# Two chunk pairs inverted side by side before the main loop, and the wide lane products on VectorE

## The chip, the cores and the metric

One core of one Trainium2 chip. The metric is the device time of one execution in microseconds; several runs are given by their median.

## What is computed

The program is a linear attention with a state matrix per head, followed by a dense feed-forward block and a mixture of eight experts. Cut to what matters:

```python
# attention: batch 4, 8 heads (32 "lanes"), 768 steps, head size 40
for t in range(S):
    y[t] = r[t] @ state
    Sa = state @ a[t]
    state = state * w[t] - outer(Sa, b[t]) + outer(v[t], k[t])
# dense block on 3072 tokens of width 320
h = x @ w_in                          # 320 -> 2048
x = where(h > 0, h, exp(min(h, 0)) - 1) @ w_out
# experts: softmax gate, best of 8, up to 768 tokens each
y = relu(x_e @ w1[e]) @ w2[e];  out = gate * y
```

## The kernel before, in words

**Tiling.** The 768 steps are cut into 24 chunks of 32 (`NCH`), taken as 12 pairs (`NP`). Within a chunk the recurrence becomes matrix products, if a 32 x 32 unit triangular matrix per lane is inverted. A pair has 64 such matrices (2 chunks x 32 lanes). Two pairs make a group of 128 steps, so there are six groups.

**`lanes` (L126)** makes, for one group, running products of the decay w inside each chunk and scales a, b and k by them. Tiles are 128 partitions (32 lanes x 4 chunks) by 32 steps by 40. The narrow steps (L166, L169, L190, L193) take 160 or 320 elements per partition, the three wide products (L174, L196, L201) 1280. For group 0 the engine `eng` is VectorE (DVE) and the tiles are separate (`room`); for groups 1 to 5 it is GpSimd (POOL), one tile `lx` takes a, b and k in turn, and loads and stores are issued by POOL. L174 runs on POOL for all six groups. The results go to DRAM.

**`pre` (L269)** of a pair: three times it takes a token tile (`turn`, L242: TensorE transposes, copies off PSUM, then the next load of the list `order`, L118), multiplies them (L288), masks the product on DVE into `TM` (L294) and stores that to `Td` in DRAM (L299), once per chunk.

**`inverse` (L308)** of a pair loads `Td` back lane-wise (L315), and in 31 steps j builds the inverse in `UL`, all on DVE: an outer product of n x m elements with n = j // 2 + 1 and m = 30 - j (L323), a multiply-add of one column (L328), an add of the outer product (L330). The result goes to `Ud` (L334) and back as `UT`, in eight loads (L339).

**`chain` (L371)** of a chunk is the serial part. Its second step (L407) multiplies by `UT`; the state that it leaves (L428, L429) is what the next chunk starts from. At its end `put` (L583) transposes the attention output into the tokens of the dense block.

**`Moe1.weights`, called conv (L494)** reads the dense weights in 40 items (per 5 items, 3 of w_in and 2 of w_out), each converted by one or two ScalarE (ACT) and five DVE instructions (L515 to L519, L480, L481); a w_out item also has transposes and small products on TensorE (L556, L560). `Moe1.block(p)` (L593) is the dense block on the 256 tokens of pair p.

**The order.** A scheduling program orders each engine's instructions by priority; `ahead` raises a generator's priority, `weave` deals generators out in a ratio. `issue_after(ins)` queues what is issued inside it behind `ins`, on the engine of `ins` alone. Each engine then runs its instructions in that fixed order. `start` (L1118) is lanes 0, `pre(0)`, `inverse(0)`, lanes 1; it is woven with 9 steps of conv. Then `pre(1)` is woven with the rest of conv, whose DVE instructions stand behind the last add of `inverse(0)` (L1152). Then comes the main loop over p (L1154): the chains of pair p, `inverse(p + 1)`, `pre(p + 2)`, a part of the lanes of a later group, and `block(p - 1)`. After it the experts follow.

Of the kernel before, what the change touches and what calls it, by code (L numbers as in the profile page):

```python
# [38 lines left out]
class Attention:  # L39
# [31 lines left out]
    def setup(self, ident, psum):  # L71
# [47 lines left out]
        for p in range(-2, NP):  # L119
            if p >= 0:  # L120
                self.order.append(("r", p))
            if p + 2 < NP:
                self.order += [("a", p + 2), ("bk", 2 * p + 4), ("bk", 2 * p + 5)]
        self.loaded = self.taken = self.banks = 0

    def lanes(self, g, eng, eng2=None, room=None):  # L126

# [3 lines left out]
        nc = self.nc  # L131
        eng2 = eng2 or eng
        W, la, wd = self.t("W"), self.t("lx"), self.t("WCd")
# [39 lines left out]
        nc.vector.tensor_copy(wd[:, 64:104], W[:, 32, :])  # L173
        nc.gpsimd.tensor_tensor(la, la, W[:, 0:32, :], ALU.mult)  # L174
        store(self.scr_A[g], la)
        if not room:
            store(self.scr_W[g], W[:, 0:32, :])
            load(W[:, 0:32, :], "w")
            load(lb, "b")
        ps = self.psum("p")  # L180
        nc.tensor.transpose(ps[0:104, 0:128], wd, self.ident)
# [10 lines left out]
        for q in range(3, -1, -1):  # L192
            eng.tensor_tensor(  # L193
                Vq[:, q], Vq[:, q], V[:, 8 * q + 8, :].unsqueeze(1).to_broadcast([128, 8, 40]), ALU.mult)
            yield
        eng2.tensor_tensor(lb, lb, V[:, 1:33, :], ALU.mult)  # L196
        store(self.scr_BK[g][:, 0:C], lb)
        if not room:
            load(lk, "k")
        yield  # L200
        self.scaled = eng2.tensor_tensor(lk, lk, V[:, 1:33, :], ALU.mult)  # L201
        store(self.scr_BK[g][:, C:2 * C], lk)
# [17 lines left out]
    def load_tok(self):  # L220

        if self.loaded == len(self.order):
            return
        kind, i = self.order[self.loaded]
        t = self.t("tok", self.loaded)
        self.loaded += 1
        for hg in range(2):
            rows = t[64 * hg:64 * hg + 64]
            if kind == "r":
                self.load_heads(rows, self.src["r"], hg, 64 * i, 64)  # L230
            elif kind == "a":
                for cc in range(2):
                    self.nc.sync.dma_start(
                        rows[32 * cc:32 * cc + 32, :, 0:40],
                        self.of(self.scr_A[i // 2], 2 * (i % 2) + cc, 16 * hg, 16).rearrange("l s d -> s l d"))
            else:

                with self.tc.issue_after(self.returned.ins) if i == 4 else ExitStack():
                    self.last = self.nc.sync.dma_start(
                        rows[:, :, 0:40], self.of(self.scr_BK[i // 4], i % 4, 16 * hg, 16).rearrange("l x d -> x l d"))  # L240
# [67 lines left out]
    def inverse(self, p):  # L308
# [27 lines left out]
        for cc in range(2):  # L336
            for b in range(4):
                h = 32 * cc + 8 * b
                self.returned = self.nc.sync.dma_start(  # L339
                    self.t("UT", 2 * p + cc)[32 * b:32 * b + 32], self.Ud[p][:, h:h + 8, :])  # L340
        yield

    def load_pv(self, c):
# [27 lines left out]
    def chain(self, c, put):  # L371
# [88 lines left out]
        if c + 2 < NCH:  # L460
            self.load_pv(c + 2)
        nc.scalar.copy(xt[:, 320:384], xt[:, 256:320])
        if not last:
# [20 lines left out]
class Moe1:  # L484
# [80 lines left out]

    def begin_x(self, ctx, i):
        pool = ctx.enter_context(self.tc.tile_pool(name=f"moe1_x{i}", bufs=1))
        self.xH.append(pool.tile([128, 3, 256], F32R, name=f"xH{i}"))
        self.xL.append(pool.tile([128, 3, 256], F32R, name=f"xL{i}"))
# [505 lines left out]
def body(ctx, tc, r, k, v, w, a, b, w_in, w_out, w_gate, w1, w2, out, capacity=768):  # L1075
# [26 lines left out]
    moe1.begin_x(st["moe1"], 1)  # L1102
    moe1.begin(st["moe1"], psum)
    put = moe1.put_x(ident, psum)
    stage = ExitStack()
    pool = stage.enter_context(tc.tile_pool(name="stage", bufs=1))
    steps = lambda t: t.rearrange("p (s d) -> p s d", d=D)
# [10 lines left out]
    def start():  # L1118
        lanes = att.lanes(0, nc.vector, room=room)
        for _ in range(25):  # L1120
            next(lanes)
            yield
        pre = att.pre(0)
        drain(lanes)
        yield from pre
        inverse = att.inverse(0)
        next(inverse)
        with tc.issue_after(att.last.ins):
            att.load_pv(0)
            att.load_bkd(0)  # L1130
            att.load_wp(0)
            att.load_pv(1)
        yield
        drain(att.lanes(1, nc.gpsimd))
        yield from inverse
# [13 lines left out]
    with tc.issue_after(att.landed.ins):  # L1149
        next(conv)  # L1150
    weave((first, 20), (behind(att.scaled.ins, some(conv, 9)), 20))
    weave((ahead(tc, att.pre(1), 1000), 10), (behind(att.inverted.ins, conv), 40))  # L1152
    lanes = None
    for p in range(NP + 1):  # L1154
        gens = []
        if p < NP:
            gens.append((ahead(tc, chained(att.chain(2 * p, put), att.chain(2 * p + 1, put)), 2000), 32))
            if p % 2 == 0:
                lanes = att.lanes(p // 2 + 2, nc.gpsimd) if p // 2 + 2 < NP // 2 else iter(())
            if p + 1 < NP:  # L1160
                gens.append((ahead(tc, att.inverse(p + 1), 1500), 20))
            if p + 2 < NP:
                gens.append((ahead(tc, att.pre(p + 2), 1500), 20, 6))
            gens.append((ahead(tc, some(lanes, 14) if p % 2 == 0 else lanes, 500 if p == 0 else 2000), 14))
        if p == 1:
            stage.close()
            moe1.begin_x(stage, 2)
        if p == NP:
# [74 lines left out]
```

## Time and profile before

| | us |
|---|---|
| median of 3 runs | 1213.22 (1212.05 to 1215.55) |
| the profiled execution, whole | 1217.03 |
| its span, first to last instruction | 1215.3 |
| PE (TensorE) matmul busy in the span | 1027.2 (85%) |
| DVE busy | 822.6 (68%) |
| ACT busy | 599.1 (49%) |
| POOL busy | 256.1 (21%) |

Busy times are of the profiled execution. PE's granted clock is 0.904 of full speed on average. An engine's share is over the whole span, and the program passes through stages with different limits, so stretches are read one by one.

### The profile page before, as it was taken

The page shows a single profiled execution, that of the slowest core. Times are in us where ns is not written, and L with a number is a line of the kernel's source. Part 1 is how long each engine was busy: PE and PEld are TensorE (multiplying, and loading weights), DVE is VectorE, ACT ScalarE, POOL GpSimd, SP SyncE. Part 2 cuts the span into 40 slices and gives each one's busy share as a digit, 9 for nine tenths or more (in the row PEclk, how much of TensorE's full clock was granted, in tenths as well). Part 3 has the DMA queues.
Part 4 walks back from the last instruction along what each step waited for, and adds up shares of the span by engine and source line. Part 5 has one row for each costly group of instructions (what it writes and reads, how often), then busy time and mean ns, then how long its engine had stood idle before and what let it go on. Part 6 is the DMA issues. An engine that isn't in the chain of part 4 may idle for free.

```text
span 1215.3 us, 35896 instructions
## 1 busy us (share of the span) xinstructions
PE 1027.2 (85%) x14568; PEld 933.5 (77%) x14568; DVE 822.6 (68%) x2755; ACT 599.1 (49%) x1499; POOL 256.1 (21%) x314
## 2 busy tenths in 40 slices
PE   0454588888988989889999979999998798989995
PEld 0344478777976988779888879888988697979995
DVE  6676798998679576968596949686445456545541
ACT  1432246564654655556556655656655345434420
POOL 5355543410035100400000000000001232323311
PEclk9855669899998989899999989999989999989998
DMA  6887667663356544452616351522131165544210
GB/s 217 205 196 217 188 166 173 194 132 65 62 103 176 104 67 81 106 104 51 108 31 101 58 104 30 91 50 44 27 88 25 39 188 159 164 134 124 82 45 22
DMA packets 294400, 131.27 MB, mean 108 GB/s; under 512 B 261560, under 2 KB 276032, under 8 KB 294224
## 3 DMA queue, kind: packets, MB, share of 16 engines
q1 hardware_dynamic: 276672, 76.39, 32.2%
q0 software_dynamic: 10064, 37.39, 9.7%
q10 hardware_dynamic: 7488, 15.09, 4.1%
q8 instruction: 117, 1.92, 0.7%
q14 instruction: 59, 0.48, 0.1%
HBM read 99.13 MB, written 31.00 MB: 107 GB/s over the span
## 4 chain that ended last, share of the span: by engine, by line
PE 41%; DVE 27%; DMA 19%; ACT 5%; issue 5%; SPq 2%; POOL 1%; ACTq 0%; POOLq 0%; DVEq 0%
PE ps_h L609 8%; PE ps_c L383 4%; DVE inv L328 4%; DVE inv L330 4%; DVE ut L323 3%; DMA out_dram<-ys,ids 3%; DMA inv<-Td 3%; PE ps_o L623 3%; PE ps_o L625 3%; PE ps_o L624 3%; PE ps_c L931 2%; DMA Td<-keep 2%; PE ps_h L931 2%; DMA r<-in_moe_w_dram 2%; DMA Ud<-inv 2%
## 5 line engine op out<-in xcount | busy, mean ns | idle before, releaser
L480 ACT CAST gH<-e 128x256 fp32r<-128x256 f32 x192 | 77.2, 405 | 116.7 <-DVE e L615 102.0
L623 PE MATMUL ps_o<-woH,gH 128*128 128x328 f32 x384 | 129.5, 340 | 5.2 <-ACT gH L480 4.5
L728 POOL DMA_INDIRECT list<-ids,idx x24 | 24.1, 1004 | 498.4 <-DVE idx L724 306.8
L624 PE MATMUL ps_o<-woL,gH 128*128 128x328 f32 x384 | 125.7, 329 | 0.0
L625 PE MATMUL ps_o<-woH,gL 128*128 128x328 f32 x384 | 120.7, 336 | 4.9 <-DVE gL L481 4.8
L615 DVE SCALAR_TENSOR_TENSOR e<-e,ps_h 128x256 f32<-128x256 f32 x184 | 76.2, 415 | 69.0 <-ACT e L614 65.5
L609 PE MATMUL ps_h<-xH,wiH 128*128 128x256 f32 x368 | 113.0, 308 | 10.4 <-DVE e L615 6.6
L323 DVE TENSOR_TENSOR ut<-inv 128x30 f32<-128x30 f32 (+4 forms) x360 | 93.2, 259 | 29.0 <-DMA inv<-Td 28.6
L609 PE MATMUL ps_h<-xL,wiH 128*128 128x256 f32 x368 | 108.6, 295 | 0.0
L609 PE MATMUL ps_h<-xH,wiL 128*128 128x256 f32 x368 | 108.5, 296 | 0.0
L328 DVE SCALAR_TENSOR_TENSOR inv<-inv 128x1 f32<-128x1 f32 (+15 forms) x372 | 101.5, 273 | 0.6
L330 DVE TENSOR_TENSOR inv<-inv,ut 128x30 f32<-128x30 f32 (+4 forms) x360 | 99.7, 277 | 0.2
L481 DVE TENSOR_TENSOR gL<-e,gH 128x256 fp32r<-128x256 f32 x192 | 81.3, 426 | 26.7 <-ACT gH L480 23.3
L253 PE MATMUL ps_p<-ident,tok 128*104 128x128 f32 x288 | 55.0, 320 | 49.4 <-DMA tok<-scr_A 24.8
L613 ACT ACTIVATE e<-ps_h 128x256 f32<-128x256 f32 x184 | 70.3, 384 | 53.4 <-PE ps_h L609 33.9
L609 PEld LDWEIGHTS ps_h<-xH,wiH 128*128 128x128 f32 x368 | 73.7, 201 | 15.0 <-DVE e L615 9.5
L623 PEld LDWEIGHTS ps_o<-woH,gH 128*128 128x128 f32 x384 | 76.8, 200 | 7.7 <-ACT gH L480 5.5
L614 ACT ACTIVATE e<-e 128x256 f32<-128x256 f32 x192 | 79.1, 417 | 4.3
L625 PEld LDWEIGHTS ps_o<-woH,gL 128*128 128x128 f32 x384 | 73.6, 199 | 7.9 <-DVE gL L481 7.2
L253 PEld LDWEIGHTS ps_p<-ident,tok 128*104 128x104 f32 x288 | 35.9, 148 | 56.4 <-issue 25.5
L624 PEld LDWEIGHTS ps_o<-woL,gH 128*128 128x128 f32 x384 | 77.1, 201 | 0.5
L609 PEld LDWEIGHTS ps_h<-xL,wiH 128*128 128x128 f32 x368 | 74.1, 201 | 0.1
(323 smaller groups left out, 2867.5 us busy)
## 6 DMA issues: line engine op xcount, KB each, us to landing
r<-in_moe_w_dram SPq DMA_DIRECT2D x15, 640.0 KB
tok<-scr_BK SPq DMA_DIRECT2D x48, 160.0 KB
BKd<-scr_BK SPq DMA_DIRECT2D x48, 160.0 KB
r<-in_moe_w_dram SPq DMA_DIRECT2D x7, 1024.0 KB
W<-in_w_dram POOLq DMA_DIRECT2D x10, 640.0 KB, 6.3
scr_BK<-lx POOLq DMA_DIRECT2D x10, 640.0 KB, 3.5
inv<-Td SPq DMA_DIRECT2D x24, 256.0 KB
raw<-in_moe_w_out_dram ACTq DMA_DIRECT2D x16, 320.0 KB
```

The source lines that it names most:

```text
L253: self.nc.tensor.transpose(ps[0:104, 128 * j:128 * j + 128], t[:, 2 * q:2 * q + 2, :].rearrange("p a e -> p (a e)")[:, 0:104], self.ident,)
L323: nc.vector.tensor_tensor(tv, TL[:, j:j + 1, j + 2:32].to_broadcast([128, n, m]), UL[:, 0:n, j:j + 1].to_broadcast([128, n, m]), ALU.mult,)
L328: nc.vector.scalar_tensor_tensor(col, UL[:, 0:n, j], TL[:, j, j + 1:j + 2], col, ALU.mult, ALU.add)
L330: self.inverted = nc.vector.tensor_tensor(UL[:, 0:n, j + 2:32], UL[:, 0:n, j + 2:32], tv, ALU.add)
L480: split.last = nc.scalar.copy(H, x)
L481: return (low or nc.vector).tensor_tensor(L, x, H.bitcast(F32), ALU.subtract)
L609: nc.tensor.matmul(h, l, r, start=i == 0, stop=i == len(seq) - 1)
L614: nc.scalar.activation(e, e, AF.Exp, scale=-1.0)
L615: nc.vector.scalar_tensor_tensor(e, e, -1.0, h, ALU.add, ALU.max)
L623: nc.tensor.matmul(o, gH[:, ts], self.woH[:, f], start=f == 0, stop=False)
L624: nc.tensor.matmul(o, gH[:, ts], self.woL[:, f], start=False, stop=False)
L625: nc.tensor.matmul(o, gL[:, ts], self.woH[:, f], start=False, stop=f == NF - 1)
```

## The change

- The opening runs `pre(0)` and `pre(1)`, and then one `inverses` for both pairs: the partitions hold chunk lanes as before, and a new free dimension q holds the two pairs. Per step j there are one outer product and one add, each over both pairs, and two multiply-adds of a column, one for each pair (its factor is a per-partition scalar). The 8 KB tile `twice` holds the input of both and is given up after conv.
- The results of pair 0 are stored and loaded first; of pair 1, the `UT` of its first chunk is loaded in the opening and that of its second in chain 0 (three `UT` buffers).
- Lanes 1 stand after the loads of `inverses` in the program; the load of token tile ("a", 2) is held until then. Their transposition takes a PSUM bank of another tag.
- In the opening 14 steps of conv are woven in, not 9; the other items stand behind the last add of `inverses`, on DVE. `inverse(1)` leaves the main loop, and from p = 1 on the loop is as before.
- The three wide products are issued to DVE in all groups; the narrow steps, loads and stores of groups 1 to 5 stay on POOL.
- Some pools change sides, and the pool of the dense block opens after `twice` is given up.

```diff
-    def lanes(self, g, eng, eng2=None, room=None):
+        self.hold = True
+    def lanes(self, g, eng, room=None):
...
-        nc.gpsimd.tensor_tensor(la, la, W[:, 0:32, :], ALU.mult)
+        nc.vector.tensor_tensor(la, la, W[:, 0:32, :], ALU.mult)
...
-        ps = self.psum("p")
+        ps = self.psum("o" if g == 1 else "p")
...
-        eng2.tensor_tensor(lb, lb, V[:, 1:33, :], ALU.mult)
+        nc.vector.tensor_tensor(lb, lb, V[:, 1:33, :], ALU.mult)
...
-        self.scaled = eng2.tensor_tensor(lk, lk, V[:, 1:33, :], ALU.mult)
+        self.scaled = nc.vector.tensor_tensor(lk, lk, V[:, 1:33, :], ALU.mult)
...
+        if self.hold and (kind, i) == ("a", 2):
+            return
...
+    def inverses(self, room):
+        nc = self.nc
+        TL = room.rearrange("p (q a b) -> p q a b", q=2, a=32)
+        UL = self.inv[:, 0:1024].rearrange("p (q a b) -> p q a b", q=2, a=16)
+        ut = [self.inv[:, 1024 + 256 * i:1280 + 256 * i] for i in range(2)]
+        nc.vector.memset(self.inv[:, 0:1024], 0.0)
+        for i in range(2):
+            half = slice(64 * i, 64 * i + 64)
+            for q in range(2):
+                self.last = self.nc.sync.dma_start(TL[half, q], self.Td[q])
+                nc.vector.memset(self.inv[half, 512 * q:512 * q + 512][:, i::34], 1.0)
+        yield
+        for j in range(31):
+            n, m = j // 2 + 1, 30 - j
+            if m:
+                tv = ut[j % 2][:, 0:2 * n * m].rearrange("p (q a b) -> p q a b", q=2, a=n)
+                nc.vector.tensor_tensor(
+                    tv, TL[:, :, j:j + 1, j + 2:32].to_broadcast([128, 2, n, m]),
+                    UL[:, :, 0:n, j:j + 1].to_broadcast([128, 2, n, m]), ALU.mult,
+                )
+            for q in range(2):
+                col = UL[:, q, 0:n, j + 1]
+                nc.vector.scalar_tensor_tensor(
+                    col, UL[:, q, 0:n, j], TL[:, q, j, j + 1:j + 2], col, ALU.mult, ALU.add)
+            if m:
+                rest = UL[:, :, 0:n, j + 2:32]
+                self.inverted = nc.vector.tensor_tensor(rest, rest, tv, ALU.add)
+            if j % 2 == 1:
+                yield
+        for p in range(2):
+            for i in range(2):
+                self.nc.sync.dma_start(
+                    self.Ud[p].rearrange("(a i) l t -> i l a t", i=2)[i], UL[64 * i:64 * i + 64, p])
+            for cc in range(2 - p):
+                self.load_ut(p, cc)
+        yield
...
+        if c == 0:
+            self.load_ut(1, 1)
...
-    moe1.begin(st["moe1"], psum)
+    moe1.psum = psum
...
+    twice = beside.enter_context(tc.tile_pool(name="beside", bufs=1)).tile([128, 2048], F32, name="twice")
...
         yield from pre
-        inverse = att.inverse(0)
+        yield from att.pre(1)
+        inverse = att.inverses(twice)
         next(inverse)
         with tc.issue_after(att.last.ins):
...
-        yield
-        drain(att.lanes(1, nc.gpsimd))
+            drain(att.lanes(1, nc.gpsimd))
+            att.hold = False
+            att.load_tok()
+        yield
         yield from inverse
...
-    weave((first, 20), (behind(att.scaled.ins, some(conv, 9)), 20))
-    weave((ahead(tc, att.pre(1), 1000), 10), (behind(att.inverted.ins, conv), 40))
+    weave((first, 26), (behind(att.scaled.ins, some(conv, 14)), 20))
+    drain(behind(att.inverted.ins, conv))
+    beside.close()
+    moe1.begin(st["moe1"], psum)
...
-            if p + 1 < NP:
+            if p > 0 and p + 1 < NP:
                 gens.append((ahead(tc, att.inverse(p + 1), 1500), 20))
```

## Rows read from the trace of the kernel before

**Rows 1.** Busy time by engine in three stretches; us, PE, PEld, DVE, ACT, POOL, PE clock, DMA.

```profile
104.00:188.00 84.00, 60.60 (x951) 52.61 (x952) 66.63 (x196) 31.12 (x84) 37.08 (x46) 0.62 0.70 185
188.00:284.00 96.00, 82.01 (x1286) 72.17 (x1284) 85.70 (x256) 58.65 (x166) 28.89 (x33) 0.93 0.67 163
284.00:420.00 136.00, 121.51 (x2159) 109.66 (x2158) 105.23 (x370) 71.96 (x188) 31.94 (x37) 0.91 0.48 103
```

**Rows 2.** The chain that ended last, 104 to 188 us; start us, us, what.

```profile
106.94 8.99 DMA Td<-keep
116.50 8.85 DMA inv<-Td
```

**Rows 3.** What PE waited for, 104 to 284 us; us in total, times, longest.

```profile
PE ps_c L383 <- DVE pv L414: 7.3, 3, 5.1
PE ps_c L383 <- DMA UT<-Ud: 6.9, 1, 6.9
PE ps_c L253 <- DVE ST L428: 5.7, 2, 5.0
```

**Rows 4.** The timeline in the opening, wide products of group 0; start us, us, what.

```profile
12.53 2.89 POOL L174 TENSOR_TENSOR lx<-lx,W 128x1280 f32<-128x1280 f32 x1 [0.24 <-DVE W L169]
12.60 3.31 DVE L172 COPY WCd<-W 128x40 f32<-128x40 f32 x1
...
19.50 1.49 DVE L196 TENSOR_TENSOR keep<-keep,inv 128x1280 f32<-128x1280 f32 x1
```

**Rows 5.** The timeline around `pre(0)`, `pre(1)` and the first inversion.

```profile
60.43 0.68 DVE L294 TENSOR_TENSOR keep<-ps_p,m_tm 128x512 f32<-128x512 f32 x1
...
64.70 1.10 PE L253 MATMUL ps_p<-ident,tok 128*104 128x128 f32 x4
...
70.55 0.19 DVE L323 TENSOR_TENSOR ut<-inv 128x30 f32<-128x30 f32 x1 [5.38 <-DMA inv<-Td]
...
72.22 1.98 PE L288 MATMUL ps_p<-Abd,BKT 104*64 104x64 f32 x32 [0.68 <-ACT BKT L275]
```

**Rows 6.** The timeline of steps of the first inversion, its last instruction, the first use.

```profile
75.64 0.20 DVE L323 TENSOR_TENSOR ut<-inv 128x54 f32<-128x54 f32 x1
...
76.02 0.23 DVE L323 TENSOR_TENSOR ut<-inv 128x78 f32<-128x78 f32 x1
...
81.52 0.29 DVE L323 TENSOR_TENSOR ut<-inv 128x128 f32<-128x128 f32 x1
81.72 0.23 DVE L328 SCALAR_TENSOR_TENSOR inv<-inv 128x8 f32<-128x8 f32 x1
81.87 0.28 DVE L330 TENSOR_TENSOR inv<-inv,ut 128x128 f32<-128x128 f32 x1
82.07 0.28 DVE L323 TENSOR_TENSOR ut<-inv 128x120 f32<-128x120 f32 x1
...
92.86 0.24 DVE L328 SCALAR_TENSOR_TENSOR inv<-inv 128x16 f32<-128x16 f32 x1
...
104.30 0.31 PE L383 MATMUL ps_c<-X,UT 32*32 32x40 f32 x2 [6.87 <-DMA UT<-Ud]
```

**Rows 7.** POOL's groups to 520 us; busy us, mean ns, idle before them, what ended it.

```profile
L193 POOL TENSOR_TENSOR W<-W 128x320 f32<-128x320 f32 x20 | 17.9, 897 | 112.9 <-DVE W L187 64.6 <-DVE at L721 47.0
...
L201 POOL TENSOR_TENSOR lx<-lx,W 128x1280 f32<-128x1280 f32 x5 | 14.7, 2931 | 18.3 <-DMA lx<-in_k_dram 18.2
```

**Rows 8.** The dense block 0 ends: PE's timeline.

```profile
283.93 0.31 PE L625 MATMUL ps_o<-woH,gL 128*128 128x328 f32 x1
```

**Rows 9.** PE and PEld busy of L560, then of L556, 104 to 284 us; as rows 1.

```profile
104.00:284.00 180.00, 15.24 (x78) 14.40 (x78) 0.78 0.68 173
...
104.00:284.00 180.00, 7.63 (x36) 4.33 (x36) 0.78 0.68 173
```

**Rows 10.** The chain that ended last, whole span: DVE pieces; start us, us, what.

```profile
367.96 2.80 DVE inv L330
...
508.71 3.10 DVE inv L328
```

More of the change, by code (lines that the diff above doesn't have):

```diff
@@ L124, in setup @@
         self.loaded = self.taken = self.banks = 0
-    def lanes(self, g, eng, eng2=None, room=None):
+        self.hold = True
+    def lanes(self, g, eng, room=None):
         nc = self.nc
-        eng2 = eng2 or eng
         W, la, wd = self.t("W"), self.t("lx"), self.t("WCd")
@@ L336, in inverse, with load_ut @@
         for cc in range(2):
[L337 to L340, printed above, removed]
+            self.load_ut(p, cc)
         yield
+    def inverses(self, room):
[32 more added lines that the diff above has]
+            for cc in range(2 - p):
+                self.load_ut(p, cc)
+        yield
+    def load_ut(self, p, cc):
+        for b in range(4):
+            h = 32 * cc + 8 * b
+            self.returned = self.nc.sync.dma_start(
+                self.t("UT", 2 * p + cc)[32 * b:32 * b + 32], self.Ud[p][:, h:h + 8, :])
     def load_pv(self, c):
@@ L564, in weights, with begin_x @@
                 yield
-    def begin_x(self, ctx, i):
-        pool = ctx.enter_context(self.tc.tile_pool(name=f"moe1_x{i}", bufs=1))
+    def begin_x(self, ctx, i, **kw):
+        pool = ctx.enter_context(self.tc.tile_pool(name=f"moe1_x{i}", bufs=1, **kw))
         self.xH.append(pool.tile([128, 3, 256], F32R, name=f"xH{i}"))
@@ L1102, in body @@
     moe1.begin_x(st["moe1"], 1)
-    moe1.begin(st["moe1"], psum)
+    moe1.psum = psum
     put = moe1.put_x(ident, psum)
     stage = ExitStack()
-    pool = stage.enter_context(tc.tile_pool(name="stage", bufs=1))
+    pool = stage.enter_context(tc.tile_pool(name="stage", bufs=1, side="right"))
+    beside = ExitStack()
+    twice = beside.enter_context(tc.tile_pool(name="beside", bufs=1)).tile([128, 2048], F32, name="twice")
     steps = lambda t: t.rearrange("p (s d) -> p s d", d=D)
@@ L1166, in body @@
             stage.close()
-            moe1.begin_x(stage, 2)
+            moe1.begin_x(stage, 2, side="right")
         if p == NP:
```

## The prediction
> **What bounds the kernel now.** I read the page's busy times first and then the stretches, because the shares over the whole span (PE 85%, DVE 68%) hide that the limit moves. In rows 1 the reader sees three stages. From 104 to 188 us, where chains 0 and 1 run before the dense block has started, PE is busy for 60.6 of 84 us at a granted clock of 0.62, and DVE for 66.6. From 188 to 284 us, the dense block 0, DVE is busy for 85.7 of 96 us and PE for 82.0, now at 0.93. From 284 on PE is busy for nine tenths and more [rows 1]. So up to 284 us DVE is the engine that is nearly full, and PE runs with holes and partly at half clock.
>
> Second I read what PE waited for there [rows 3]: 7.3 us for DVE's scaling of pv, 5.7 us for DVE's update of ST, 6.9 us for the return of the first inverse. Third the chain that ended last: between 107 and 125 us it is no engine at all but the second pair's trip through DRAM, 8.99 us out and 8.85 us back [rows 2], and then `inverse(1)` on DVE. Fourth the timeline beside a wide POOL product: a DVE copy that begins at 12.60, with POOL's product running from 12.53 to 15.42, takes 3.31 us [rows 4]. Later pieces of 2.8 to 3.1 us of single small inversion instructions stand in the chain that ended last for the same reason; four of them come after 360 us, the first and the last are shown [rows 10].
>
> **The change, part by part.** The sum is made against the profiled execution, 1217.0 us whole; the median of the runs, 1213.2, is 3.8 us below it, and at the end I take the difference off the median.
>
> *Wide products.* One on DVE takes 1.49 us [rows 4], one on POOL 2.93 [rows 7], and while that runs DVE gets one instruction through, in about 2.8 to 3.1 us. So each move takes some 1.4 us off DVE, though it adds an instruction there. In the opening it is direct: 3.31 us become 1.49 and a short copy, which I put at 0.2, about the length of the small column instruction [rows 6]. Gain 1.6, and I take 1.5, as the token loads behind it are DMAs.
>
> On this point the Trainium skill speaks against the change: Perfetto Trace Analysis, section Optimizing Scalar/DVE Operations, says that when DVE is saturated, moving some work to ScalarE or even GpSimd may make sense, and adds that DVE and GpSimd share a port, so that moves between these two might not help. By its first half each move back to DVE would cost the 1.49 us; the 3.31 us copy [rows 4] stands for the second half, and by that row the sum has a gain.
>
> *The inversion starts later.* The mask of `pre(0)`'s second chunk ends at 60.43 + 0.68 = 61.1 us [rows 5]. Less 1.5 from the opening and 1.5 for the wide product of group 1, which lies in that stretch: 58.1. `pre(1)` then runs undivided. From its first transposes at 64.70 to the end of its first L288 group at 72.22 + 1.98 = 74.2 it took 9.5 us, then a mask of 0.7. The second chunk has one token tile instead of two (half of 72.22 - 64.70, 3.8 us), the products of 2.0 and a mask of 0.7. Together 58.1 + 9.5 + 0.7 + 6.5 = 74.8. Out to DRAM and back took 70.55 - 61.1 = 9.4 us [rows 5]; four loads instead of two, I take 10.5. The inversion starts at about 85.3 us instead of 70.55. The other bound is the slow trip, 17.8 us [rows 2]: 93. I keep near the lower one, since conv is held back to 14 items and little else loads then.
>
> *The inversion itself.* A single step with 54 elements takes 76.02 - 75.64 = 0.38 us from start to start, one with 128 takes 82.07 - 81.52 = 0.55 [rows 6]. The elements n x m sum to 2600 over 31 steps, 84 on average, which makes 0.45 us a step, 14.0 for all. Side by side, a step gets its elements twice (2.3 ns for each in the two wide instructions, 0.19 us) and a second column instruction (81.87 - 81.72 = 0.15): 0.79 us, 24.5 for all, against 28.0 for two. No row shows an instruction over two pairs; the bounds are 14 (as one) and 28 (as two). Inside lie two wide products (3.0), and the narrow POOL steps of group 2 hold DVE: ten at about 0.9 us [rows 7], of which I charge half, 5, between none and 9. So it ends at 85.3 + 24.5 + 8 = 117.8, where the first one ended at 93.1. The trip by Ud and UT took 104.3 - 93.1 = 11.2 us [rows 6], so chain 0's product with UT comes at 129.0 instead of 104.3: **24.7 us late**.
>
> *What comes back behind it.* The stretch from there to the end of block 0 was 284.2 - 104.3 = 180 us [rows 6, 8], PE busy for 142.6 [rows 1]. It now has no second trip through DRAM, no `inverse(1)` (14 us of DVE and more with its stalls), and the six wide products of groups 2 and 3 at 1.4 less: DVE's 152 us become some 130. Conv is ahead: 13 w_out items were left in the stretch [rows 9]; 14 items before the inversion ends and some four before 129 us leave 10. Three at 15.24 / 13 + 7.63 / 12 = 1.8 us of PE: 5.4 off, 137.2 left. The idle 37.4 us lose the wait for UT (6.9) and the two for DVE (13.0) [rows 3]: 17.5. With fewer holes the clock of the first part should lie between its 0.62 and the 0.93 of the next stretch [rows 1]; I take 0.75, so 55.2 us there become 45.6. The stretch is then 137.2 - 9.6 + 17.5 = 145.1 us, and block 0 ends at 274.1, **10.1 us earlier**.
>
> *Later.* Four locked pieces on the chain [rows 10] give up 1.4 each, 5.8. PE is already busy for 121.5 of 136 us there [rows 1], so some of it is hidden: 4. The remaining products, the moved UT load (four small loads behind others on SP, needed three chains later), the other PSUM tag and the pools' sides I cost at nothing: POOL's waits are long [rows 7], and lanes run two pairs ahead of their use. If that lead were gone, POOL's stores would wait for DVE and the next `pre` with them.
>
> Sum: -10.1 - 4 = -14.1, or 1203 for an execution like the profiled one, **1199 for the median**.
>
> **The rivals.** *The clock comes up at once, faster still.* Chains 0 to 3 run with all inverses at hand, so PE could be granted 0.93 from the start [rows 1]: 55.2 us become 36.8 (8.8 less than I took), POOL's narrow steps miss the inversion (5 less), another 5 of idle time go, and all of the 5.8 is had. About 1179. Against it: PE has little to do until the first UT product, and it had 0.62 where it had holes.
>
> *DVE waits where POOL waited.* POOL stood idle for 18.2 us in four waits for the load of k ahead of L201 [rows 7], which cost nothing there; on DVE, whose order is fixed, the same late load stops everything behind it: the inversion and the chains' updates. At 4.5 us for each of five groups, half on the path, 11 us come back: 1210. For it: DVE already waited for returning loads [rows 5]. Against it: in the trace DVE's reciprocal made POOL wait, for 64.6 us in all [rows 7], so the order tends to put DVE's part late.
>
> *The late start is not made up, slower.* The 24.7 us are certain, the return is not. If the chains are bound by their own sequence, PE keeps 0.62 and all its idle time but the wait for UT: 137.2 + 30.5 = 167.7, block 0 ends at 296.7, 12.5 late, and with the later 4 the median is 1222. It decides once the stretch from the first UT product to the end of block 0 is longer than 284.2 - 129.0 + 4 = 159 us.
>
> *The moved work simply loads the full engine, slower.* Then ten products on the path cost 1.49 instead of giving 1.4, 29 us more than I took: 1228. The 3.31 us copy speaks against it [rows 4]. That is the skill's rule above.
>
> **How the numbers follow.** My forecast has 0.44 (its own range 1189 to 1209), the clock 0.15, DVE's waits 0.14, the late start 0.23, the loaded engine 0.04. A measurement of this kernel can tell about 0.3%, 3.6 us, from no change. Faster: 0.44 + 0.15 + 0.04 of DVE's waits = 0.63. The same (1209.6 to 1216.9): the other 0.10 of these and 0.02 of the late start = 0.12. Slower: 0.25. The range 1180 to 1224 leaves out half of the clock case and the far part of the two slow ones, under 0.2.
>
> **What would show it.** Right: no DVE instruction of about 3 us beside a POOL product; the inversion begins near 85 and takes about 32 us with what lies inside; the first product with UT near 129; block 0 ends before 280; DVE's wait before the wide products is small. Wrong: the first UT product after 140, PE's clock near 0.6 up to the dense block, DVE idle before L196 or L201 on a load, or a dense block 0 that still waits for conv.

## The result, and the profile after

The changed kernel takes **1228.6 us** (median of 4 runs, 1225.1 to 1234.5) against 1213.5 of the kernel before beside it: 1.0109 times, 95% interval 1.0068 to 1.0150. It is slower, by 15 us, where 14 us were to be gained. The profiled execution is the fastest of the four, 1225.1 us with a span of 1223.3; that of the kernel before took 1217.0, 3.5 us above that median. In the spans, then, only 8 of the 15 us can be seen.

First the stretches, as in [rows 1] (us, then PE, PEld, DVE, ACT, POOL busy, PE's granted clock, DMA share, GB/s), of the changed kernel:

```profile
104.00:146.00 42.00, 3.52 (x14) 2.55 (x14) 36.65 (x131) 3.18 (x9) 12.46 (x19) 0.50 0.45 133
146.00:207.00 61.00, 48.47 (x944) 42.27 (x944) 42.49 (x97) 31.00 (x83) 13.60 (x23) 0.83 0.78 181
207.00:296.00 89.00, 74.00 (x1243) 66.55 (x1244) 73.20 (x227) 50.46 (x138) 19.30 (x30) 0.92 0.62 149
296.00:420.00 124.00, 112.64 (x1991) 100.77 (x1990) 97.77 (x366) 69.86 (x187) 23.35 (x34) 0.96 0.48 106
```

and the first 42 us of that in the kernel before:

```profile
104.00:146.00 42.00, 25.78 (x355) 22.18 (x355) 30.86 (x93) 12.84 (x36) 20.39 (x23) 0.56 0.66 190
```

Look at PE in the first line of each: 3.5 us of work in 42 where there were 25.8. DVE is busy for 36.7 of them, with the inversion. From 146 us on the changed kernel is the denser one: in 61 us before dense block 0 PE is busy for 48.5, at 0.83, where [rows 1] had 60.6 in 84 at 0.62.

Next the timeline of the changed kernel from `pre(1)` to the first product with UT, against [rows 5, 6] (start us, us, engine, line, what; in brackets the idle time ahead of it and its releaser). L290 is the product of `pre`, L296 its mask, L561 to L564 conv's instructions on DVE, L601 a transposition of conv on PE, L352 the load of both pairs' matrices, L359, L365 and L369 the three instructions of a step of the inversion, L426 the chain's product:

```profile
68.15 1.98 PE L290 MATMUL ps_p<-Abd,BKT 104*64 104x64 f32 x32 [1.34 <-ACT BKT L277]
...
72.76 0.49 DVE L561 SCALAR_TENSOR_TENSOR xf<-xf,raw 128x320 f32<-128x320 f32 x1 [0.39 <-ACT xf L560]
73.17 0.68 DVE L296 TENSOR_TENSOR keep<-ps_p,m_tm 128x512 f32<-128x512 f32 x1
...
73.91 1.09 PE L255 MATMUL ps_p<-ident,tok 128*104 128x128 f32 x4 [3.78 <-DVE keep L296]
...
75.09 0.22 DVE L365 SCALAR_TENSOR_TENSOR inv<-inv,twice 128x1 f32<-128x1 f32 x1 [1.00 <-DMA twice<-Td]
...
81.76 0.69 DVE L296 TENSOR_TENSOR keep<-ps_p,m_tm 128x512 f32<-128x512 f32 x1 [3.21 <-PE ps_p L290]
...
85.33 1.49 DVE L201 TENSOR_TENSOR lx<-lx,W 128x1280 f32<-128x1280 f32 x1 [2.33 <-DMA lx<-in_k_dram]
...
87.31 1.13 SPq L352 DMA_DIRECT2D twice<-Td  x2
...
96.36 4.29 POOL L166 TENSOR_TENSOR W<-W 128x160 f32<-128x160 f32 x7 [3.89 <-DMA W<-in_w_dram]
...
96.68 0.27 DVE L359 TENSOR_TENSOR inv<-twice,inv 128x60 f32<-128x60 f32 x1 [9.85 <-DMA twice<-Td]
...
102.93 0.97 DVE L359 TENSOR_TENSOR inv<-twice,inv 128x150 f32<-128x150 f32 x1
...
113.35 0.41 DVE L359 TENSOR_TENSOR inv<-twice,inv 128x256 f32<-128x256 f32 x1
113.68 0.37 DVE L365 SCALAR_TENSOR_TENSOR inv<-inv,twice 128x8 f32<-128x8 f32 x2
113.96 0.42 DVE L369 TENSOR_TENSOR inv<-inv 128x256 f32<-128x256 f32 x1
114.30 0.41 DVE L359 TENSOR_TENSOR inv<-twice,inv 128x240 f32<-128x240 f32 x1
...
133.88 0.26 DVE L365 SCALAR_TENSOR_TENSOR inv<-inv,twice 128x16 f32<-128x16 f32 x2
...
136.58 0.91 PE L601 MATMUL ps_r<-ident,x 128*128 128x128 f32 x3 [29.64 <-DVE x L564]
...
145.99 0.88 PE L426 MATMUL ps_c<-X,UT 32*32 32x40 f32 x6 [6.35 <-DMA UT<-Ud]
```

Read it from the bottom. The first product with UT begins at 145.99 us instead of 104.30 [rows 6], 41.7 us late. Ahead of it PE stood for 29.6 us before a transposition of conv (L601): PE's order had put that item next, and its DVE part (L564) stands behind the last add of the inversion. The inversion ran from 96.68 to 134.14, 37.5 us. It began 9.85 us after DVE's last work, on the loads of `Td`; the second mask of `pre(1)` had ended at 82.45. Pair 0's input had landed by 75.09, when DVE ran the first column of pair 0 (L365); the paired product (L359) came 21.6 us later, with pair 1's.

Dense block 0 (L654 begins it, L670 ends it; compare [rows 8]) of the changed kernel:

```profile
207.40 0.50 PE L654 MATMUL ps_h<-xH,wiH 128*128 128x256 f32 x2 [1.27 <-ACT xH L525]
```

```profile
295.82 0.32 PE L670 MATMUL ps_o<-woH,gL 128*128 128x328 f32 x1
```

Block 0 ends at 296.1, 11.9 us after 284.2. At the end of block 5 the two kernels are level (633.8 and 634.4), at the end of block 11 the changed one is 8.6 late (961.2 and 952.6), and so it ends. What PE waited for in these last stretches (us in total, times, longest), in the changed kernel, 634 to 961 us:

```profile
PE ps_p L255 <- DMA tok<-scr_A: 8.4, 2, 4.3
PE ps_c L426 <- DVE GN L484: 5.6, 2, 5.3
PE ps_p L950 <- issue: 4.9, 1, 4.9
PE ps_o L668 <- ACT gH L525: 3.4, 1, 3.4
```

and in the kernel before, 634 to 953 us:

```profile
PE ps_p L253 <- DMA tok<-scr_A: 6.7, 1, 6.7
PE ps_p L905 <- issue: 3.5, 1, 3.5
PE ps_o L623 <- ACT gH L480: 2.4, 2, 1.4
...
PE ps_c L383 <- DVE GN L441: 1.3, 1, 1.3
```

There is no new kind of wait, only single ones of 3 to 5 us that are longer or fall elsewhere. Of the diff only the places of the pools reach into these stages, and the order of the instructions, which the scheduling program made anew; both kernels have three UT buffers (L110), and the wide products have all been issued by 520 us.

Last the wide products (busy us, mean ns, idle ahead of them) to 520 us, against [rows 7]:

```profile
L174 DVE TENSOR_TENSOR lx<-lx,W 128x1280 f32<-128x1280 f32 x6 | 8.8, 1470 | 0.0
L201 DVE TENSOR_TENSOR lx<-lx,W 128x1280 f32<-128x1280 f32 x5 | 7.5, 1493 | 5.9 <-DMA lx<-in_k_dram 5.8
L196 DVE TENSOR_TENSOR lx<-lx,W 128x1280 f32<-128x1280 f32 x5 | 7.4, 1482 | 0.0
```

They take 1.47 to 1.49 us, as on DVE before, and wait for the load of k for 5.8 us in all, not 18.2.

### The profile page after: what moved, and what is told of

Its sections match the earlier page's. It is cut to its first block, busy times and chain, and to the rows that moved or that the text cites. A ratio compares the mean times of both kernels' runs of the same rounds, so it can differ in the third digit from the quotient of the medians.

```text
span 1223.3 us, 35861 instructions
## 1 busy us (share of the span) xinstructions
PE 1007.8 (82%) x14568; PEld 918.2 (75%) x14568; DVE 810.4 (66%) x2710; ACT 598.9 (49%) x1499; POOL 210.2 (17%) x298
## 4 chain that ended last, share of the span: by engine, by line
PE 35%; DMA 24%; DVE 21%; issue 9%; ACT 4%; SPq 3%; POOL 2%; POOLq 0%; ACTq 0%; DVEq 0%
PE ps_h L654 7%; PE ps_c L426 5%; DMA out_dram<-ys,ids 4%; DMA raw<-in_moe_w_in_dram 3%; PE ps_o L668 3%; PE ps_o L670 3%; PE ps_o L669 3%; DVE ut L325 2%; DVE inv L332 2%; DMA xs<-rows,ids 2%; DVE inv L330 2%; DMA list<-ids,idx 2%; PE ps_r L426 2%; DVE e L660 2%; PE ps_p L255 1%
## 5 line engine op out<-in xcount | busy, mean ns | idle before, releaser
L670 PE MATMUL ps_o<-woH,gL 128*128 128x328 f32 x384 | 120.8, 334 | 2.3 <-DVE gL L526 2.1
L660 DVE SCALAR_TENSOR_TENSOR e<-e,ps_h 128x256 f32<-128x256 f32 x184 | 76.5, 416 | 64.9 <-ACT e L659 63.6
L654 PE MATMUL ps_h<-xH,wiH 128*128 128x256 f32 x368 | 110.5, 302 | 6.8 <-DVE e L660 5.5
L654 PE MATMUL ps_h<-xL,wiH 128*128 128x256 f32 x368 | 107.8, 293 | 0.0
L654 PE MATMUL ps_h<-xH,wiL 128*128 128x256 f32 x368 | 107.5, 292 | 0.0
L526 DVE TENSOR_TENSOR gL<-e,gH 128x256 fp32r<-128x256 f32 x192 | 81.2, 427 | 28.4 <-ACT gH L525 24.7
L325 DVE TENSOR_TENSOR ut<-inv 128x120 f32<-128x120 f32 (+4 forms) x300 | 74.8, 249 | 17.7 <-DMA inv<-Td 17.5
L255 PE MATMUL ps_p<-ident,tok 128*104 128x128 f32 x288 | 52.4, 309 | 40.3 <-DMA tok<-scr_A 16.7
L654 PEld LDWEIGHTS ps_h<-xH,wiH 128*128 128x128 f32 x368 | 72.1, 197 | 10.2 <-DVE e L660 7.5
L670 PEld LDWEIGHTS ps_o<-woH,gL 128*128 128x128 f32 x384 | 73.3, 197 | 4.5 <-DVE gL L526 3.2
L332 DVE TENSOR_TENSOR inv<-inv,ut 128x120 f32<-128x120 f32 (+4 forms) x300 | 74.0, 247 | 0.3
L330 DVE SCALAR_TENSOR_TENSOR inv<-inv 128x1 f32<-128x1 f32 (+15 forms) x310 | 73.8, 238 | 0.5
L654 PEld LDWEIGHTS ps_h<-xH,wiL 128*128 128x128 f32 x368 | 72.6, 197 | 0.4
L654 PEld LDWEIGHTS ps_h<-xL,wiH 128*128 128x128 f32 x368 | 72.6, 197 | 0.2
```

Of the source, the lines that this page charges most:

```text
L325: nc.vector.tensor_tensor(tv, TL[:, j:j + 1, j + 2:32].to_broadcast([128, n, m]), UL[:, 0:n, j:j + 1].to_broadcast([128, n, m]), ALU.mult,)
L330: nc.vector.scalar_tensor_tensor(col, UL[:, 0:n, j], TL[:, j, j + 1:j + 2], col, ALU.mult, ALU.add)
L332: self.inverted = nc.vector.tensor_tensor(UL[:, 0:n, j + 2:32], UL[:, 0:n, j + 2:32], tv, ALU.add)
L526: return (low or nc.vector).tensor_tensor(L, x, H.bitcast(F32), ALU.subtract)
L654: nc.tensor.matmul(h, l, r, start=i == 0, stop=i == len(seq) - 1)
L660: nc.vector.scalar_tensor_tensor(e, e, -1.0, h, ALU.add, ALU.max)
```

## The experiments

Ratios are to the kernel before on the same chip, with 95% intervals. Milestones are read from each profile's timeline.

**The two halves of the change, each alone.** *wide_only* is the kernel before with L174, L196 and L201 on DVE; *la_only* moves L174 alone; *pair_only* is the changed kernel with the three back on POOL; *one_by_one* is the changed kernel with the pairs inverted one after the other, pair 0 first and sent off before pair 1 starts.

```diff
# wide_only (la_only: the first line of the three alone)
-        nc.gpsimd.tensor_tensor(la, la, W[:, 0:32, :], ALU.mult)
+        nc.vector.tensor_tensor(la, la, W[:, 0:32, :], ALU.mult)
-        eng2.tensor_tensor(lb, lb, V[:, 1:33, :], ALU.mult)
+        nc.vector.tensor_tensor(lb, lb, V[:, 1:33, :], ALU.mult)
-        self.scaled = eng2.tensor_tensor(lk, lk, V[:, 1:33, :], ALU.mult)
+        self.scaled = nc.vector.tensor_tensor(lk, lk, V[:, 1:33, :], ALU.mult)
# one_by_one
-        for j in range(31):
+        for p in range(2):
+            for j in range(31):
...
-                    tv, TL[:, :, j:j + 1, j + 2:32].to_broadcast([128, 2, n, m]),
+                        tv, TL[:, p, j:j + 1, j + 2:32].to_broadcast([128, n, m]),
```

> The kernel before with nothing but the three wide products on DVE; the opening and the inversions are as they were. Theory A, the late start is the loss: the products alone are a gain, 1200 to 1208 us, and no DVE instruction of about 3 us is left beside a POOL product. Theory B, DVE waits in order for what POOL used to wait for: 1217 us or more, with DVE idle ahead of L174, L196 and L201.

> The kernel before with only the product L174 on DVE, L196 and L201 of groups 1 to 5 left on POOL. Theory A: a third of the gain of all three, 1207 to 1211 us, most of it from the opening. Theory B, where the load of k ahead of L201 is the harm: no worse than before, 1209 to 1214, so that the harm of all three together must come from L196 and L201.

> The changed kernel with the three wide products back on POOL (group 0 but for L174 on DVE as before): the side-by-side inversion alone. Theory A: slower than the changed kernel, 1235 us or more, as the late start stays and the products' gain goes. Theory B: 1213 to 1222, faster than the changed kernel's 1228.

> The changed kernel with its opening order (both pre first, same tiles, same loads), but the two inversions one after the other, single-pair instructions, the result of pair 0 stored and loaded before pair 1 is begun. Theory A, the start of chain 0 sets the loss: its first UT product comes 12 us or more earlier than the changed kernel's 146, at 125 to 134, and the time falls to 1214 to 1221. If the start of chain 0 is not what counts, the longer DVE work (3 us) leaves it at 1226 to 1234.

Measured: wide_only 0.9845 (0.9771 to 0.9919; its six runs spread from 1187.5 to 1219.2 us and their median is 0.994 times, so that *wide_again* below is the figure to go by), la_only 1.0057 (1.0029 to 1.0085), pair_only 1.0148 (1.0106 to 1.0190), one_by_one **0.9936** (0.9906 to 0.9965). So the products do not load a full engine, all three together are a gain. In this comparison the loss goes with the side-by-side inversion, and without it the rest of the change is faster than the kernel before; the next experiments limit both halves of that sentence. one_by_one came to its first product with UT sooner than expected (108.2 us), and that L174 alone is a small loss, which neither theory had, is not explained.

**Is it the paired instructions, or the time at which pair 0 is ready?** *pair1_first* is one_by_one with the order of the pairs turned round: not one paired instruction, but chain 0 again gets its inverse last. *conv9* is the changed kernel with 9 items of conv in the opening, as before. *conv_behind0* is one_by_one with conv held behind the last add of pair 0 only. *wide_again* repeats wide_only.

```diff
# pair1_first
-        for p in range(2):
+        for p in (1, 0):
# conv9
-    weave((first, 26), (behind(att.scaled.ins, some(conv, 14)), 20))
+    weave((first, 26), (behind(att.scaled.ins, some(conv, 9)), 20))
# conv_behind0
-                    self.inverted = nc.vector.tensor_tensor(rest, rest, tv, ALU.add)
+                    add = nc.vector.tensor_tensor(rest, rest, tv, ALU.add)
+                    if p == 0:
+                        self.inverted = add
```

> The one-by-one kernel with pair 1 inverted before pair 0: the same instructions, loads and stores, another order, so that only chain 0's start moves. Theory A, the start of chain 0 sets the loss: its first UT product comes at 130 to 146 us instead of 108, block 0 ends 8 to 15 us later than one by one, the offset stays to the end, and the time is 1218 to 1230. Theory C, the paired instructions themselves are what is slow: as one by one, 1203 to 1212, since no instruction here is over two pairs.

> The changed kernel with 9 steps of conv woven into the opening instead of 14. If conv's work is what delays the second pre, the mask of its second chunk ends nearer 75 than the changed kernel's 82.4 us, the first UT product comes 4 to 8 us earlier than 146 and the time is 1220 to 1226; but conv has more left afterwards. If the DRAM trip and the inversion set the start anyway: 1226 to 1234.

> The one-by-one kernel with the rest of conv standing on DVE behind pair 0's last add, not pair 1's, so that it runs beside the second inversion. If DVE's order after the first inversion is free, this starts the dense weights earlier and the time is 1198 to 1206; if chain 0 and 1 then wait for conv on DVE, 1208 to 1216.

> The kernel before with the wide products alone on DVE, beside the others on the same chip, since its first timing was spread over 30 us. Theory A: 1200 to 1210 us, level with one by one. If the first timing's lowest run was the true one: below 1195.

Measured: pair1_first **1.0140** (1.0073 to 1.0208), conv9 1.0128 (1.0074 to 1.0183), conv_behind0 0.9988 (0.9961 to 1.0016), wide_again 0.9926 (0.9885 to 0.9966). The inversion of pair 0 (its first and its last instruction) and the first product with UT in one_by_one, then the first product with UT in pair1_first:

```profile
76.00 0.18 DVE L360 TENSOR_TENSOR inv<-twice,inv 128x30 f32<-128x30 f32 x1
...
99.72 0.24 DVE L365 SCALAR_TENSOR_TENSOR inv<-inv,twice 128x16 f32<-128x16 f32 x1
...
108.18 0.31 PE L425 MATMUL ps_c<-X,UT 32*32 32x40 f32 x2 [2.18 <-DMA UT<-Ud]
```

```profile
139.51 0.90 PE L600 MATMUL ps_r<-ident,x 128*128 128x128 f32 x3 [33.42 <-DVE x L563]
141.03 1.55 PE L604 MATMUL ps_r<-wg,raw 128*128 128x8 f32 x6 [0.62 <-ACT raw L602]
144.63 0.34 PE L425 MATMUL ps_c<-X,UT 32*32 32x40 f32 x2 [2.05 <-DMA UT<-Ud]
```

Alone, with no other input to wait for, the inversion of pair 0 runs from 76.0 to 100.0 us; in the changed kernel the paired one ran from 96.7 to 134.1. The same instructions in the other order put chain 0 back by 36.5 us and PE behind conv for 33.4, and the kernel is as slow as the changed one: the paired instructions are not what costs. But pair1_first is no clean test of the start either. Its block 0 ends at 286.2, only 4.7 us after one_by_one's, where 8 to 15 were expected, and its block 5 at 641.4, 23 us after; and between the ends of blocks 5 and 11 DVE, which runs the same sequence in both executions of one_by_one, runs another one here. Two results do not fit a theory of the start alone. conv9 begins 9 us sooner than the changed kernel (137.1) and gains nothing; its block 0 ends at 300.9, which would fit the conv that it has left, but that was not tried by itself. conv_behind0 has block 0 done at 256.8, 27 us before the kernel before, has lost it by the end of block 1 (345.9 against 342.5), and is 5 us late at the end of block 5 (639.4): the end of a block alone does not tell how far the chains are.

**The products once more, and repeats.** *obo_pool* is one_by_one with the three products back on POOL (the lines of wide_only, turned round); *after_again*, *one_by_one_again* and *before_again* are repeats.

> The one-by-one kernel with the wide products back on POOL: the new opening order without the pairing and without the products' move, the fourth corner beside the changed kernel, the pairing alone and one by one. Theory A: the order alone costs little, ratio to before 0.995 to 1.006, so that the pairing's price is 1 to 2 per cent with and without the products. If the order itself (both pre first) is the harm, 1.008 or more.

> The changed kernel again, to see whether its pace late in the main loop belongs to its order: in its first profile it had drawn level with before when block 5 ended (634 us in both) and lost 9 us from there to the end of block 11. If that is its order: again 6 us or more lost there against the kernel before. If it is this execution: 3 or less. Ratio 1.007 to 1.015 in both cases.

> The one-by-one kernel beside the changed one and the kernel before on the same chip: ratio 0.990 to 0.997, block 11 ending 12 to 25 us ahead of the changed kernel's, which is the distance that is already there when block 0 ends.

> The kernel before, profiled a second time. If its fast pace between the ends of blocks 5 and 11 (634 to 953 us, 318 us in the first profile) belongs to its order: 316 to 321 again; if it was that execution: 323 to 330, as the other kernels took.

Measured: obo_pool **1.0195** (1.0148 to 1.0242), after_again 1.0140 (1.0101 to 1.0180), one_by_one_again 0.9945 (0.9913 to 0.9977); before_again, a single run, 1215.4 us. The repeats hold: between the ends of blocks 5 and 11 the kernel before takes 318.9 us (318.2 the first time) and the changed one 333.6 (327.4), so what is lost there belongs to the kernel and not to one execution. obo_pool is the surprise: 4 us ahead of the kernel before at the end of block 0 (280.1), 9 us late at the end of block 5 and 27 at the end of block 11 (979.1), and the last 17 of these are lost where no instruction differs. By its own expectation this is the result of the rival, that the opening order (both `pre` first) is the harm. And with the products on POOL, undoing the pairing gains nothing: 1.0195 against 1.0148 of pair_only, although the first product with UT comes at 119.0 instead of 144.9. With the products on DVE the same opening order is one_by_one, at 0.994. So neither the pairing nor the opening order has a price that holds in both. The three pairs of kernels that differ in the products alone all go the same way: wide_only against before by 0.7% (wide_again; the first timing had 1.6), the changed kernel against pair_only by 0.1 and 0.4%, which is within the spread of the runs, one_by_one against obo_pool by 2.5%. That is one sign and three sizes, so something else sets the size.

**The order of the loop.** Any edit of the opening also reshuffles the fixed order of everything behind it. To see what that is worth, two numbers that have nothing to do with the change were altered, from p = 3 on, in the kernel before, the changed one and one_by_one:

```diff
# before_i, after_i, one_i
-                gens.append((ahead(tc, att.inverse(p + 1), 1500), 20))
+                gens.append((ahead(tc, att.inverse(p + 1), 1500 if p < 3 else 1700), 20))
# before_b, after_b, one_b
-            gens.append((moe1.block(p - 1, route.tile), 42))
+            gens.append((moe1.block(p - 1, route.tile), 42 if p < 3 else 36))
```

> The kernel before, with one number changed that has nothing to do with the change: from p = 3 on the inverse's priority is 1700 instead of 1500, so that the static order of the main loop is another one from about the inverse of pair 4 on, and the opening and dense blocks 0 and 1 are as they were. Theory start (the late start of chain 0 costs the 20 us between the changed kernel and the one that inverts one by one): the order of the loop is worth little, so within 5 us of the kernel before. Rival order (which order of the loop the program happens to get decides): 5 to 15 us away, to either side.

> The changed kernel with the same number changed (inverse 1700 from p = 3 on). Theory start: as the changed kernel, 1.010 to 1.016 times the kernel before, and 14 to 26 us above the one-by-one kernel with the same number changed. Rival order: the distance to that kernel is another one, under 10 us or over 30.

> The kernel that inverts the two pairs one by one with the products on DVE, with the same number changed (inverse 1700 from p = 3 on). Theory start: 0.990 to 0.998 times the kernel before, as without it. Rival order: its lead was a lucky order and is gone: 1.000 or more.

> The kernel before with another number changed: from p = 3 on the share of the dense block among the generators is 36 instead of 42, so that the order of the main loop is another one from about dense block 2 on. Theory start: within 5 us of the kernel before. Rival order: 5 to 15 us away, to either side.

> The changed kernel with the same number changed (block's share 36 from p = 3 on). Theory start: 1.010 to 1.016 times the kernel before and 14 to 26 us above the one-by-one kernel with the same number changed. Rival order: that distance is under 10 us or over 30.

> The one-by-one kernel with the same number changed (block's share 36 from p = 3 on). Theory start: 0.990 to 0.998 times the kernel before. Rival order: 1.000 or more, or below 0.985.

Measured, with the milestones in us (first product with UT, ends of blocks 0, 5 and 11, span) of the profiled executions:

| kernel | UT | block 0 | block 5 | block 11 | span | ratio (95%) |
|---|---|---|---|---|---|---|
| before | 104.3 | 284.2 | 634.4 | 952.6 | 1215.3 | 1 |
| before_i | 101.0 | 280.9 | 630.4 | 947.0 | 1220.8 | 1.0003 (0.9964 to 1.0041) |
| before_b | 104.6 | 286.0 | 630.6 | 951.2 | 1212.2 | 0.9995 (0.9963 to 1.0027) |
| after | 146.0 | 296.1 | 633.8 | 961.2 | 1223.3 | 1.0109 (1.0068 to 1.0150) |
| after_i | 146.3 | 296.5 | 641.5 | 977.5 | 1243.0 | 1.0159 (1.0108 to 1.0210) |
| after_b | 141.5 | 294.5 | 626.5 | 950.9 | 1208.6 | 1.0044 (1.0021 to 1.0068) |
| one_by_one | 108.2 | 281.5 | 618.4 | 939.5 | 1200.0 | 0.9936 (0.9906 to 0.9965) |
| one_i | 109.9 | 277.9 | 623.5 | 947.7 | 1211.9 | 0.9998 (0.9958 to 1.0038) |
| one_b | 109.7 | 284.1 | 620.0 | 945.0 | 1210.0 | 1.0004 (0.9976 to 1.0031) |

Both theories have a part, and neither is shown alone. The start: in all three orders the changed kernel is slower than the kernel before, and than one_by_one by 1.7 and 1.9% in two runs, by 1.6%, and by 0.4%, which the spread of the runs does not tell from nothing. Its block 0 ends 10 to 19 us after one_by_one's, and its block 5 still 6.5 to 18. Against the kernel before, however, the late start has been made up when block 5 ends, in the order as it was (0.6 us ahead, in the repeats 2.7 late) and in the second shuffle (4.1 ahead), and only in the first it has not (11.1 late): that the late start is what costs the 15 us at the end is not shown. The order: behind block 5 the changed kernel takes 589.5 us (span less block 5's end; 592.7 in the repeat), 601.5 or 582.1, one_by_one 581.6 to 590.0. These are single executions, and not all stand near their median: after_i's took 1244.9 us, with a median of 1235.3, after_b's 1210.4, with 1218.6. In the medians the 24 us between the two kernels (1234.2 and 1210.0 on one chip) became 18 in one shuffle and 3 in the other (1235.3 and 1217.0, 1218.6 and 1215.6). And the lead of one_by_one over the kernel before, 0.6% in two runs, is gone in both shuffles: it belongs to one order, not to the edit. Why one order goes faster than another was not found; the profile shows only single waits of PE, of 3 to 7 us, at other places: between the ends of blocks 5 and 11 after_i waits 7.6 us for DVE's e (L660) where the changed kernel waits 1.4, and 0.3 us for GN, where that has 5.6. Whether the late start alone, with every later order kept, costs anything at the end was not tried.

## Why the prediction was wrong, point by point

| step | forecast | measured |
|---|---|---|
| second mask of `pre(0)` ends | 58.1 | 57.0 |
| second mask of `pre(1)` ends | 74.8 | 82.5 |
| inversion starts | 85.3 | 96.7 |
| its length | 32.5 | 37.5 |
| first product with UT | 129.0 | 146.0 |
| from there to the end of block 0 | 145.1 | 150.1 |
| block 0 ends | 274.1 | 296.1 |
| from there to the end of the program, less than before | 4 | 3.9 |

The sum fell **in the step "the inversion starts later"**: 24.7 us late was forecast, 41.7 came, and these 17.0 with the 5.0 of the stretch behind it are the whole 22 us by which the profiled execution missed 1203. The forecast's own sign of being wrong, a first product with UT after 140, came. The other 7 us of the median's miss (1228.6 for 1199) lie in where the two profiled executions stand among their runs.

The trip through `Td` ahead of the inversion, as the chain that ended last shows it, first in the kernel before and then in the changed one:

```profile
61.49 3.79 DMA Td<-keep
65.86 4.66 DMA inv<-Td
```

```profile
82.82 4.34 DMA Td<-keep
...
87.83 8.82 DMA twice<-Td
```

- *`pre(1)`, 7.6 too short (the forecast's 74.8 against 82.5).* I said that it runs undivided. It does not: 14 items of conv are dealt in, and DVE works in a fixed order. The first product (L290) ended at 70.13, and its mask began at 73.17, behind conv's instructions (L561 ahead of it in the timeline); the transposition of the next token tile (L255, 73.91) then waited 3.78 us for that mask. With 9 items (conv9) the second mask ended at 79.6.
- *The trip through Td, 3.7 too short.* From the mask to the first step 14.2 us, not 10.5. The load of `Td` is what grew, 8.82 us instead of 4.66. I left the slow bound, 17.8, aside because little else would load. The DMA engines were not free: their share was 0.91 from 82 to 97 us. But it was 1.05 from 61 to 71 us in the kernel before, so the share does not say why this load took twice as long; that stays open.
- *The inversion, 5.0 too short.* A paired step where POOL is idle takes 114.30 - 113.35 = 0.95 us with 256 elements, by my formula 1.0: that part was right. But POOL's narrow steps beside it were 21, not ten, and took 4.29 + 3.00 us to 103.7 (L166, L169) and 8.94 from 119.1 (L190, L193); there L359 takes 0.97 us for 150 elements and 0.41 for 256 without. I had counted only L193's length of 0.9, not the steps of 160 elements, which hold DVE too. From start to start the steps took 32.3 us, 2.8 more than 24.5 + 5; 2.3 more went to DVE's other instructions ahead of the last column (three of conv's, L561, with 1.2 of it; copies, a reciprocal, zeroing), which the sum did not have.
- *The return trip* was right (11.9 for 11.2), and so was **the return behind it** in kind: 150.1 us, not 180, without the second trip and `inverse(1)`. PE's work in it was 122.5 us, 5 less than forecast, its idle time 27.5, 10 more; 6.8 us of that were for ACT's copy of S (L517), a wait that none of my rows had.
- *Later, 4 us.* The number is right by luck, and its reason is not. The changed kernel won 12 us between the ends of blocks 0 and 5 and lost 9 between those of blocks 5 and 11. The second I put down to the order of the loop, which no step of the prediction had: besides the places of the pools nothing else differs there, and behind block 5 the time of single executions also moved by 7 to 12 us under an edit that does nothing. Which instructions of that order cost it was not found.
- *The products* cost what was said, and no DVE instruction of about 3 us is left beside one. Of the three pairs of programs two gain beyond the spread of the runs, though what of that is the order was not tried. The Trainium skill (Perfetto Trace Analysis, Optimizing Scalar/DVE Operations) says that moving work between DVE and GpSimd might not help, as they share a port; with 1.49 us on DVE [rows 4] against 2.93 on POOL [rows 7], and a DVE copy that took 3.31 us beside such a product [rows 4], these runs agree as to a move to POOL.

Of the rivals, *the late start is not made up* came nearest, block 0 at 296.1 where it had 296.7, the median at 1228.6 where it had 1222. That block 0 fits so well is luck: it got there by the start and not by its own condition, a stretch of over 159 us, and the late start was made up by the end of block 5 (633.8 against 634.4), to be lost again behind it. That I gave it 0.23 was the misjudgement: the terms of the 24.7 were taken near their lower ends, and they stand one behind the other, so that their misses could only add up. *DVE waits where POOL waited* did not matter: the waits of 2.33 and 3.29 us before L201 fell where DVE had nothing to do (the inversion was not loaded; UT was on its way). *The loaded engine*, 29 us more, is refuted by the three pairs of kernels. The clock came up to 0.83 in the first stretch, above my 0.75; by my own scaling that makes 41.2 us of the 45.6, most of the 5 us by which PE's work fell short, and the longer idle time took it back.

## What to carry to other kernels

Two producers run side by side save instructions, but the first consumer then waits for the second producer's input and for twice the work: price such a merge at the first consumer, and along a serial path take each term from a row where the engines beside it are busy, not from the quietest one. And in a program whose order is fixed by a scheduler every edit reshuffles what comes after; before a difference of 1% is put down to the edit, change the order by something that means nothing, in both kernels, and see what is left of it.

## What was not expected of the hardware

POOL's narrow steps hold DVE as the wide products do. In the changed kernel two column instructions took 0.69 us beside the steps of 160 elements (seven of them 4.29 us, L166 above), 0.99 beside those of 320 (three of them 3.00), and 0.34 with nothing beside; the outer product beside those of 320 took 0.97:

```profile
98.78 0.69 DVE L365 SCALAR_TENSOR_TENSOR inv<-inv,twice 128x2 f32<-128x2 f32 x2
...
100.72 3.00 POOL L169 TENSOR_TENSOR W<-W 128x320 f32<-128x320 f32 x3
...
101.79 0.99 DVE L365 SCALAR_TENSOR_TENSOR inv<-inv,twice 128x3 f32<-128x3 f32 x2
...
103.82 0.34 DVE L365 SCALAR_TENSOR_TENSOR inv<-inv,twice 128x3 f32<-128x3 f32 x2
```

The granted clock can differ twofold where PE does the same work: from 104 to 146 us the changed kernel shows 0.50 (1.2 GHz) with 3.52 us of PE work, and pair1_first, here from 104 to 145, 1.00 (2.4 GHz) with 3.85:

```profile
104.00:145.00 41.00, 3.85 (x15) 2.73 (x15) 37.41 (x168) 1.96 (x6) 11.77 (x19) 1.00 0.52 154
```

The changed kernel had no matrix product from 84 to 97 us before that, pair1_first had 45 of them, 1.04 us in all, all but one from 95.8 us on; why the one stretch shows 0.50 and the other 1.00 stays open. The three transpositions of conv in it took 0.91 and 0.90 us all the same, so for them the column does not show in the time.
